# A fused retention and low-rank MLP kernel on one core: which queue stores the first 384 columns of the last output row block

## The chip, the cores and the metric

The kernel runs on one core of one Trainium2 chip. The time is that of one execution on the device, in microseconds (us); the number quoted is the median over several executions. One further execution was taken by the hardware profiler, and all durations below are from it.

## The reference

Two stages are joined. The first is a linear attention with decay, over four batches, eight heads, 768 positions and 64 values to a head; the second is a token mixer of low rank followed by an MLP.

```python
def _attn_ref(q, k, v):                      # B, H, S, D = 4, 8, 768, 64
    for t in range(S):
        state = gamma * state + k[:, :, t] (outer) v[:, :, t]
        y[:, :, t] = scale * q[:, :, t] @ state

def _moe_ref(x, U, V, w_ch1, w_ch2):         # x: 4 x 768 x 512
    h = xt @ U @ V                           # rank 32, over the 768 positions
    u = x + h.transpose(0, 2, 1)
    ch = np.maximum(u @ w_ch1, 0.0) @ w_ch2  # 512 -> 2048 -> 512
    return u + ch
```

All inputs and the output (4 x 768 x 512) are float32 in memory. The matrix products are done in bfloat16 with float32 sums.

## The kernel before, in words

The work is written out in one order by hand. Each batch's output has 768 rows, cut into six row blocks of 128 (`NCK` is 6). For a batch, `mlp_pieces` makes a list of pieces: first the products with `w_ch1` (`up`, `up_two`, lines 429 and 442), whose results pass through a relu into `gT`; then the products with `w_ch2` (`down`, line 458). For a row block `j`, sixteen matmuls, in four pieces of four, add up in one bank of PSUM. After the last of them VectorE adds `u` to the sum and puts the float32 result into `o_sb` (line 465). Then the block is stored in the output in DRAM.

`weave` puts these pieces in order, with the attention of the next batch between them. The last batch has no next one: its end is only the six row blocks of `down`, one after the other.

The stores are made in two ways. For a whole row block, `down` puts the store into a list (line 470), and `store` (line 408) issues it on GpSimd's queue (POOL) one piece later in the written order; at the end `weave` empties the list. The very last row block, batch 3 and `j` = 5, is cut in two by columns: columns 0 to 383 (`n0` = 0, `nn` = 384), then columns 384 to 511 (`n0` = 384, `nn` = 128). It is sixteen matmuls of 384 columns, a sum on VectorE and a store, then sixteen matmuls of 128 columns, a sum and a store. Before the change the first part goes the way of all others, over the list and GpSimd. The second is issued by SyncE (SP) directly, on line 468. In what follows the first part's store is called A (128 rows of 1536 bytes, 192 KB) and the second's B (128 rows of 512 bytes, 64 KB).

SyncE's queue carries the loads of q, k and v and the transposes done by DMA; its last one before the stores was issued some 37 us before the end. GpSimd's queue carries the loads of the weights and all other stores. Behind the kernel's own instructions each engine has the program's closing ones, which the profile puts on line 860: SyncE waits for the semaphores of all DMAs, every engine passes a DRAIN, and GpSimd waits until all engines have reported and then releases them, twice.

Of the kernel before, what the change touches and what calls it, by code (L numbers as in the profile page):

```python
# [16 lines left out]
def kernel(  # L17
# [13 lines left out]
    B, H, S, D = q.shape  # L31
    NCK = S // P
# [27 lines left out]
    def bank(tag, dtype=fp32):  # L60
        n_bank[0] += 1
        return psum.tile([P, 2048 // (4 if dtype == fp32 else 2)], dtype,
                         tag=tag, name=f"{tag}_{n_bank[0]}", bufs=BANKS[tag])
# [346 lines left out]
    def mlp_pieces(b):  # L410
        gT = gtp.tile([P, NM, S], bf16, tag="gT", name=f"gT_{b}")
        pieces = []
        n = [0]

        def relu(dst, src):
            n[0] += 1
            if n[0] % 3 == 0:
                nc.vector.tensor_relu(dst, src)  # L418
            else:
                nc.scalar.activation(dst, src, AF.Relu)  # L420

        def up(m, lo, sz):
            def f():
                g_p = begun.pop((b, m, lo), None)
                c0 = 3 if g_p is not None else 0
                if not c0:
                    g_p = bank("mlp")
                for c in range(c0, NCB):
                    nc.tensor.matmul(g_p[:, :sz], w1b[:, c, ts(m, P)],  # L429
                                     uTs[b][:, c, ds(lo, sz)], start=(c == 0),  # L430
                                     stop=(c == NCB - 1))
                relu(gT[:, m, ds(lo, sz)], g_p[:, :sz])
            return f

        for m in range(NM):
            pieces.append((0.864, up(m, 0, LO)))
        def up_two(m):
            def f():
                g_p = bank("mlp")
                for n in range(2):  # L440
                    for c in range(NCB):
                        nc.tensor.matmul(g_p[:, ts(n, S - LO)], w1b[:, c, ts(m + n, P)],  # L442
                                         uTs[b][:, c, LO:], start=(c == 0),
                                         stop=(c == NCB - 1))
                relu(gT[:, ds(m, 2), LO:], g_p.rearrange("p (n t) -> p n t", n=2))
            return f

        for m in range(0, NM, 2):
            pieces.append((0.864, up_two(m)))
        hold = {}  # L450

        def down(j, m0, n0=0, nn=DM):
            def f():
                if m0 == 0:
                    hold[j, n0] = bank("mlp")
                ch = hold[j, n0]
                for m in range(m0, m0 + 4):
                    nc.tensor.matmul(ch[:, :nn], gT[:, m, ts(j, P)],  # L458
                                     w2b[:, m, ds(n0, nn)],
                                     start=(m == 0), stop=(m == NM - 1))  # L460
                if m0 == NM - 4:
                    o_sb = outp.tile([P, DM], fp32, tag="o_sb",
                                     name=f"o_{b}_{j}_{n0}")[:, :nn]
                    n = ds(n0, nn)
                    nc.vector.tensor_tensor(o_sb, ch[:, :nn], us[b][:, j, n],  # L465
                                            op=ALU.add)
                    if n0:
                        nc.sync.dma_start(out=out[b, ts(j, P), n], in_=o_sb)
                    else:
                        stores.append((nc.gpsimd, out[b, ts(j, P), n], o_sb))  # L470
            return f

        for j in range(NCK):
            if (b, j) == (B - 1, NCK - 1):
                for n0, nn in ((0, 384), (384, 128)):
                    for m0 in range(0, NM, 4):
                        pieces.append((0.864 * nn / DM, down(j, m0, n0, nn)))
                continue
            for m0 in range(0, NM, 4):
                pieces.append((0.864, down(j, m0)))  # L480
        return pieces
# [383 lines left out]
```

## Time and profile before

| | |
|---|---|
| median of 3 runs | 226.62 us (225.92 to 226.64) |
| the profiled execution's own time | 224.54 us |
| its span, first to last instruction | 222.7 us |
| TensorE (PE) busy | 214.2 us, 96% of the span |
| VectorE (DVE) / ScalarE (ACT) / GpSimd (POOL) busy | 96.7 / 82.9 / 80.0 us |
| stores of whole row blocks by GpSimd | 23, 256 KB each, 2.5 us from issue to landing |
| store A, by GpSimd | 192 KB, 2.2 us from issue to landing |
| store B, by SyncE | 64 KB, 2.0 us from issue to landing |

A row of a timeline gives start, duration, engine, line and operation. A "q" behind an engine (SPq, POOLq) means the engine's sequencer, which handles semaphores, DRAINs and DMA issues; these don't count as busy time. "q0 software_dynamic" is the DMA queue that GpSimd fills and "q1 hardware_dynamic" the one that SyncE fills; both are worked off by the core's same 16 DMA engines. What lies between the span and the execution's own time, 1.84 us here, is not seen in the records.

### The profile page before, as it was taken

Reading aid. Unit: us, or ns where it says so; the run is one execution under the profiler, and the core shown is the slowest. Engines: PE = TensorE matmul, PEld = TensorE weight load, DVE = VectorE, ACT = ScalarE, POOL = GpSimd, SP = SyncE. Lnnn points to the kernel's source line nnn. Section 1 sums busy time; section 2 is a strip of 40 time slices with the busy share of each in tenths; the row PEclk is TensorE's granted clock in tenths of the full one; section 3 lists DMA queues with packets and bytes.
Section 4 is the critical chain, followed back from the end, with each engine's and each line's share of the span. In section 5 each row is a group of like instructions: output and inputs, shape, how many; then the busy total and the mean of one; then the engine's idle time right before and its main releaser. Section 6 shows DMA issues by size and latency. Waiting matters only on the chain.

```text
span 222.7 us, 4746 instructions
## 1 busy us (share of the span) xinstructions
PE 214.2 (96%) x1955; PEld 122.7 (55%) x1982; DVE 96.7 (43%) x137; ACT 82.9 (37%) x157; POOL 80.0 (36%) x115
## 2 busy tenths in 40 slices
PE   7999999999999999999999999999999999999991
PEld 2567444865665544587444444686544444864451
DVE  6678636235635346625516145251633332222111
ACT  3776454463563244565030044745120144420000
POOL 5588661125750079370101496710111100001010
PEclk9999999999999999999999999999999999999998
DMA  6999999997989996599997644411114330001211
GB/s 175 329 308 243 204 221 200 196 249 172 294 211 259 287 247 138 123 206 203 211 281 185 176 130 96 95 26 24 50 49 150 89 94 0 0 3 47 94 74 68
DMA packets 89301, 34.58 MB, mean 155 GB/s; under 512 B 71216, under 2 KB 87728, under 8 KB 89280
## 3 DMA queue, kind: packets, MB, share of 16 engines
q1 hardware_dynamic: 83152, 23.86, 46.4%
q0 software_dynamic: 6128, 10.42, 18.3%
q8 instruction: 15, 0.25, 0.5%
q14 instruction: 6, 0.05, 0.1%
HBM read 27.46 MB, written 6.29 MB: 152 GB/s over the span
## 4 chain that ended last, share of the span: by engine, by line
PE 56%; issue 31%; POOL 5%; SPq 3%; DMA 2%; DVE 1%; ACT 1%; POOLq 0%; DVEq 0%; ACTq 0%
PE mlp L458 19%; PE mlp L429 17%; PE mlp L442 6%; POOL out_dram L408 3%; SPq L106 2%; DMA in<-in_v_dram 2%; PE r L281 2%; PE r L302 1%; PE st L313 1%; PE r L297 1%; POOL vd L83 1%; PE r L639 1%; PE r L344 1%; PE r L624 1%; PE r L584 1%
## 5 line engine op out<-in xcount | busy, mean ns | idle before, releaser
L458 PE MATMUL mlp<-w2b,gT 128*128 128x512 bf16 (+2 forms) x384 | 86.6, 370 | 1.0 <-issue 0.3
L420 ACT ACTIVATE gT<-mlp 128x512 bf16<-128x512 f32 x64 | 38.1, 597 | 69.9 <-PE mlp L429 57.1
L458 PEld LDWEIGHTS <-gT 128*128 128x128 bf16 x400 | 36.9, 98 | 38.6 <-issue 0.2
L429 PE MATMUL mlp<-uT,w1b 128*128 128x512 bf16 x243 | 56.1, 379 | 0.3
L408 POOL DMA_DIRECT2D out_dram<-o x24 | 13.3, 553 | 105.0 <-DVE o L465 97.3
L418 DVE TENSOR_SCALAR gT<-mlp 128x512 bf16<-128x512 f32 x32 | 22.1, 690 | 46.2 <-PE mlp L429 23.9
L429 PEld LDWEIGHTS <-w1b 128*128 128x128 bf16 x250 | 23.6, 98 | 27.4 <-issue 0.3
L465 DVE TENSOR_TENSOR o<-mlp,u 128x512 f32<-128x512 f32 (+2 forms) x25 | 16.8, 670 | 45.1 <-PE mlp L458 44.4
L442 PE MATMUL mlp<-uT,w1b 128*128 128x256 bf16 x256 | 29.6, 273 | 0.3 <-ACT gT L420 0.2
L442 PEld LDWEIGHTS <-w1b 128*128 128x128 bf16 x256 | 24.7, 98 | 4.2 <-issue 0.4
L284 DVE TENSOR_TENSOR a<-r,mask 128x1024 bf16<-128x1024 f32 x18 | 21.2, 1219 | 7.0 <-PE r L281 7.0
L83 POOL TENSOR_TENSOR vd<-in,gk 128x512 bf16<-128x512 f32 x18 | 18.7, 1040 | 11.8 <-DMA in<-in_v_dram 11.7
L70 ACT ACTIVATE x<-r 128x512 bf16<-128x512 f32 x20 | 11.9, 596 | 26.1 <-PE r L302 25.8
L351 DVE TENSOR_TENSOR u<-r,x 128x512 bf16<-128x512 f32 (+1 forms) x16 | 14.5, 951 | 3.6 <-PE r L344 3.6
L83 POOL TENSOR_TENSOR qd<-in,gq 128x512 bf16<-128x512 f32 x12 | 12.5, 1041 | 0.0
L81 POOL CAST kd<-in 128x512 bf16<-128x512 f32 x16 | 9.7, 611 | 7.3 <-issue 6.2
L70 ACT ACTIVATE nsz<-st 64x256 bf16<-64x256 f32 x30 | 11.2, 372 | 0.3
L83 POOL TENSOR_TENSOR qp<-in,gq 128x512 bf16<-128x512 f32 x6 | 6.2, 1046 | 6.3 <-DMA in<-in_q_dram 6.3
L591 DVE TENSOR_TENSOR a<-r,mask 128x1024 bf16<-128x1024 f32 x6 | 7.3, 1222 | 2.1 <-PE r L584 2.1
L302 PE MATMUL r<-vd,a 128*128 128x64 bf16 x144 | 7.1, 193 | 0.0
L302 PEld LDWEIGHTS <-a 128*128 128x128 bf16 x144 | 6.0, 98 | 0.7
L297 PEld LDWEIGHTS <-qT 128*128 128x128 bf16 x60 | 4.6, 98 | 2.7
(109 smaller groups left out, 151.7 us busy)
## 6 DMA issues: line engine op xcount, KB each, us to landing
in<-in_k_dram SPq DMA_DIRECT2D x24, 256.0 KB, 5.0
in<-in_q_dram SPq DMA_DIRECT2D x24, 256.0 KB, 4.8
in<-in_v_dram SPq DMA_DIRECT2D x24, 256.0 KB, 4.7
out_dram<-o POOLq DMA_DIRECT2D x23, 256.0 KB, 2.5
w1b<-in_moe_w_ch_dram POOLq DMA_DIRECT2D x4, 512.0 KB, 8.1
w2b<-in_moe_w_ch_dram POOLq DMA_DIRECT2D x4, 512.0 KB, 16.1
kT<-kd SPq DMA_TRANSPOSE x12, 2.8
qT<-qd SPq DMA_TRANSPOSE x12, 2.4
```

Source lines behind the costliest of these rows:

```text
L70: nc.scalar.activation(dst, src, AF.Copy)
L83: e.tensor_tensor(dst, src, scale, op=ALU.mult)
L284: nc.vector.tensor_tensor(a, r.rearrange("p i (n m) -> p i n m", n=4), mask[:, None, None, :].to_broadcast([P, 2, 4, P]), op=ALU.mult)
L302: nc.tensor.matmul(o[:, ts(h, D)], a[:, i, hp], vb[:, h], start=(ci == 0 and h == 0), stop=True, skip_group_check=True)
L351: nc.vector.tensor_tensor(v4(us[b][:, ds(j0, nj), e]), R[g][:, :, :nj * P].rearrange("p c (j e) -> p c j e", j=nj), v4(xs[b][:, ds(j0, nj) ...
L408: eng.dma_start(out=dst, in_=src)
L418: nc.vector.tensor_relu(dst, src)
L420: nc.scalar.activation(dst, src, AF.Relu)
L429: nc.tensor.matmul(g_p[:, :sz], w1b[:, c, ts(m, P)], uTs[b][:, c, ds(lo, sz)], start=(c == 0), stop=(c == NCB - 1))
L442: nc.tensor.matmul(g_p[:, ts(n, S - LO)], w1b[:, c, ts(m + n, P)], uTs[b][:, c, LO:], start=(c == 0), stop=(c == NCB - 1))
L458: nc.tensor.matmul(ch[:, :nn], gT[:, m, ts(j, P)], w2b[:, m, ds(n0, nn)], start=(m == 0), stop=(m == NM - 1))
L465: nc.vector.tensor_tensor(o_sb, ch[:, :nn], us[b][:, j, n], op=ALU.add)
```

## The change

The condition for the direct store on SyncE is no longer "the second part of a cut row block", but "the last row block of the last batch". As only that row block is cut, B stays where it was, and A moves from the list and GpSimd's queue to SyncE's queue, ahead of B. All other stores stay on GpSimd.

```diff
                     nc.vector.tensor_tensor(o_sb, ch[:, :nn], us[b][:, j, n],
                                             op=ALU.add)
-                    if n0:
+                    if (b, j) == (B - 1, NCK - 1):
                         nc.sync.dma_start(out=out[b, ts(j, P), n], in_=o_sb)
                     else:
                         stores.append((nc.gpsimd, out[b, ts(j, P), n], o_sb))
```

## The prediction

> **What bounds the kernel now.** The page gives TensorE 96% of the span, but the change touches nothing before the last sum. So I read only the end, first in the chain of waits (start, duration, what), cut to the last microseconds:
>
> ```profile
> 215.71 0.02 POOLq L408
> 215.73 0.54 POOL out_dram L408
> 216.27 1.90 issue
> 218.17 0.56 POOLq L860
> ```
>
> The chain ends on GpSimd's side: its last store, then its sequencer on line 860, the program's close. The timeline of the end gives the order of events:
>
> ```profile
> 217.34 0.56 DVE L465 TENSOR_TENSOR o<-mlp,u 128x384 f32<-128x384 f32 x1 [1.91 <-PE mlp L458]
> 218.19 0.54 POOL L408 DMA_DIRECT2D out_dram<-o  x1 [1.92 <-DVE o L465]
> 218.23 0.29 DVE L465 TENSOR_TENSOR o<-mlp,u 128x128 f32<-128x128 f32 x1 [0.34 <-PE mlp L458]
> 218.55 0.37 SPq L468 DMA_DIRECT2D out_dram<-o  x1
> ```
>
> A's sum stands at 217.90, GpSimd issues A 0.29 us later. B's sum stands at 218.52, SyncE issues B 0.03 us later. Then line 860 alone (durations minimum, median, maximum; first and last start):
>
> ```profile
> L860 SPq EVENT_SEMAPHORE  x11: 17/28/28, 220.4 to 222.7; - x11
> L860 POOLq EVENT_SEMAPHORE  x4: 17/17/17, 221.8 to 222.6; - x4
> L860 POOLq DRAIN  x3: 46/93/3557, 218.2 to 222.2; - x3
> L860 SPq DRAIN  x3: 7/7/7, 220.9 to 222.0; - x3
> ```
>
> This is the row that matters. One GpSimd DRAIN takes 3.557 us, 218.17 to 221.73; the two others take 0.09 and 0.05 us. At 221.77 GpSimd's first semaphore instruction meets all engines. By the records behind this view SyncE passes its last DRAIN before that meeting at 221.00: it was ready 0.73 us before GpSimd. From 221.77 to the end, 222.74, is 0.97 us of closing, the same for any path.
>
> Last, the DMA engines in windows around the two stores (the last two columns are their busy share and GB/s):
>
> ```profile
> 217.90:219.30 1.40, 0.29 (x6) 0.12 (x3) 0.29 (x1) 0.00 (x0) 0.54 (x1) 1.00 0.00 0
> 219.30:219.78 0.48, 0.00 (x0) 0.00 (x0) 0.00 (x0) 0.00 (x0) 0.00 (x0) 1.00 0.96 397
> 219.78:220.15 0.37, 0.00 (x0) 0.00 (x0) 0.00 (x0) 0.00 (x0) 0.00 (x0) 1.00 0.67 194
> ```
>
> The second window holds 48 packets, all of GpSimd's queue (A); in the third 144 of 160 are SyncE's (B). So A's first packet comes 1.12 us after its issue, and B moves only when A has left the engines, 1.23 us after its own. By the records A has landed at 220.37 and B at 220.55.
>
> **The change, part by part.** *Removed from GpSimd: one DMA issue, 0.54 us, and what its DRAIN waits for.* Nothing else is queued there. The trace shows no second long DRAIN, so its cause must be bounded. It ends 3.00 us after the end of A's issue and 1.36 us after A's landing. GpSimd's last DMA is now the store of row block 4, issued 215.72 to 216.27, landed at 218.27 by the records. The DRAIN then ends at 216.27 + 3.00 = 219.27 or 218.27 + 1.36 = 219.63. Both are over a microsecond before SyncE is ready, so either way it leaves the path. If instead it waits for every DMA of the core, it stays at 221.7; I take the first reading, since the other DRAINs with no GpSimd store before them are below 0.2 us, and keep the other as a rival. What is late next is SyncE; with nothing else changed that is worth 0.73 us.
>
> *Added to SyncE: A's wait, then its issue.* SyncE is idle before it. A starts at 217.90 + 0.03 = 217.93 and, at B's price of 0.37 us (the same 128 rows), ends at 218.30. Behind the new wait stand only B and the close; B's sum stands at 218.52, so A's issue is hidden by 0.22 us, and would cost all that it takes above 0.59 us.
>
> *A's transfer.* SyncE's first packets on idle engines come 1.03 us after the issue (the load of V at 0.74) to 1.18 us (the transposes at 168.58 and 178.75), and at most 1.23 us (B). From 1.18: A's first packet at 219.11. SyncE's packets of 512 bytes take 27 ns and of 3072 bytes 127 ns in the packet records; a row of A is 1536 bytes, on the line between them 67 ns, and eight rows to each of 16 engines make 0.54 us (0.22 to 1.02 by the two rows). The engines start 0.15 us apart, as they do before, so A is through at 219.65 to 219.80.
>
> *B's transfer.* Issued at 218.55 as before; first packet 1.03 to 1.23 us later, 219.58 to 219.78. That is when A ends, so A costs B nothing; with 127 ns packets A ends by 220.28 and B is late by 0.4 us. B's packets and landing then take what they took, 0.34 us and 0.43 us: landed at 220.35 to 220.55. I take 220.45.
>
> The Trainium skill ("DMA: Bandwidth & Descriptors", Specifications) states a first byte after about 0.6 us for SyncE's queue and about 1 us for GpSimd's; no row of SyncE here is below 1.03. By that page, as an estimate, B would land near 219.9 and the change gain about 1.7 us. Against the change speaks another page of the Trainium skill ("Trainium Kernel Development and Optimization", Key Constraints): DMAs of SP, ACT and POOL share the same 16 engines, and issuing from several at once saves only the sequencer's issue time. By it the move brings nothing in data movement and gives up the parallel issue; the windows agree on the sharing (A at 397 GB/s, then B), and the rule says nothing on the DRAIN.
>
> *SyncE's list of waits.* Before, its first closing wait starts at 220.39, 0.02 us after A's landing; nine waits about 0.06 us apart and two DRAINs follow, to 221.00. So 0.62 us of list stand behind a landing. The operands in the records name the semaphores: the first wait holds that of GpSimd's last store, the eighth B's. SyncE uses eight in turn, so A takes B's old one and B the next, which is the ninth and last of the list. The other eight are then walked before B lands, and only 0.02 us, one wait and the DRAINs remain: 0.14 us. The program may order its list otherwise; at worst B is at its head, and 0.62 us remain.
>
> **The sum**, against the profiled span of 222.74: B landed 220.45, SyncE's DRAIN 220.59, GpSimd's meeting 0.05 later at 220.64 instead of 221.77: −1.13 us (−1.03 to −1.23 by B's landing). The span becomes 221.61 and that execution's 224.54 becomes 223.41. Its own time lies 2.08 us below the median of the three runs; the difference applied to the median, 226.62 − 1.13, gives 225.5.
>
> **The rivals.** *The list is walked after B's landing.* SyncE is ready at 221.07, the meeting at 221.12: −0.65 us, 225.97. For it: that is how the list ran before. Against it: the fixed order by semaphore. A's packets at 127 ns end near the same place, −0.73 us.
>
> *The DRAIN follows the last landing of any queue.* It ended 1.18 us after B's landing, the last before; B at 220.35 to 220.55 gives a DRAIN to 221.53 to 221.73, −0.2 to 0.0 us, and if the 1.36 us behind A's landing is the constant, up to +0.18: about 226.5. For it: the one long DRAIN can't tell. Against it: SyncE's own DRAINs take 7 ns, and GpSimd's started with its own last issue.
>
> *Slower: A's issue blocks SyncE.* An issue there is not always 0.37 us: a transpose took 2.07 us at 147.69, and a load with a full queue 5.81 us at 26.33. All beyond 0.59 us delays B. With B's landing 2.00 us after its issue and 0.19 us to the meeting, the new path passes the old one from an issue of 1.65 us on; at 2.07 us it is 0.4 us slower, at 5.81 us 4.2 us, 230.8. Against it: the queue has been empty for 37 us, and issues of the same 128 rows are short.
>
> *The change does less than it says*: no; only the last row block is cut, so the two conditions differ for A alone.
>
> **How the numbers follow.** Forecast 0.70, list after the landing or slow packets 0.12, DRAIN by any landing 0.13, blocked issue 0.05. About 0.3%, 0.68 us, is what a measurement of this kernel can tell from no change. The forecast lies beyond it, but by less than the spread of the three runs, 0.72 us, so some of its share falls to "same"; the list rival lies just inside, the DRAIN rival wholly. Faster 0.68, same 0.24, slower 0.08. The range goes from the forecast's far end less a spread, 226.62 − 1.23 − 0.72 = 224.7, to the DRAIN rival with its bound, 226.62 + 0.18 = 226.8. The forecast's own range is 225.0 to 226.0.
>
> **What would show it.** Right: no 3.56 us DRAIN that ends after 220; A's issue on SyncE at 0.03 us after its sum and 0.37 us long; B's issue still 0.03 us after its sum, landed by 2.0 us; SyncE's last closing wait starting with B's landing; GpSimd's meeting within 0.1 us of SyncE's DRAIN, some 2.1 us after B's issue instead of 3.2. Wrong: a GpSimd DRAIN that still ends after SyncE's, nine waits behind B's landing, B's issue late behind A's, or B's packets late behind A's.

## The result, and the profile after

The changed kernel took 224.32 us (median of ten runs, 223.51 to 226.88); the kernel before, run beside it to ten runs in all, 225.74 us (224.92 to 226.99). The ratio is 0.9931 with a 95% interval of 0.9903 to 0.9959: faster by 0.69%, some 1.6 us (0.9 to 2.2). The ratio leaves out one of the changed kernel's ten runs, 226.88 us, as it lies more than 1.5% above the fastest. The profiled execution took 223.51 us with a span of 221.7 us.

The chain of waits, cut to the last microseconds (start, duration, what), no longer has GpSimd in it:

```profile
204.96 13.65 PE mlp L458 x79
218.61 0.02 issue
218.63 0.29 DVE o L465
```

The timeline of the end:

```profile
216.13 0.54 POOL L408 DMA_DIRECT2D out_dram<-o  x1 [2.91 <-DVE o L465]
217.74 0.56 DVE L465 TENSOR_TENSOR o<-mlp,u 128x384 f32<-128x384 f32 x1 [1.91 <-PE mlp L458]
218.33 0.98 SPq L468 DMA_DIRECT2D out_dram<-o  x2
218.63 0.29 DVE L465 TENSOR_TENSOR o<-mlp,u 128x128 f32<-128x128 f32 x1 [0.33 <-PE mlp L458]
```

The two issues of SyncE stand in one row: A at 218.33, 0.03 us after its sum, B at 218.95, 0.03 us after its own. The last sum ends at 218.93; before it ended at 218.52. The 0.4 us between the two profiles arose long before the change, and so the ends are best compared from the end of the last sum on. Line 860 (durations minimum, median, maximum; first and last start):

```profile
L860 SPq EVENT_SEMAPHORE  x11: 17/28/28, 219.4 to 221.7; - x11
L860 POOLq EVENT_SEMAPHORE  x4: 17/17/17, 220.8 to 221.6; - x4
L860 POOLq DRAIN  x3: 46/93/3588, 216.1 to 221.2; - x3
L860 SPq DRAIN  x3: 7/7/7, 220.7 to 221.0; - x3
```

The long DRAIN is still there, 3.588 us long, but it starts at 216.11 and ends at 219.70, about a microsecond before SyncE's own DRAINs at 220.68 and 220.74. The meeting is at 220.77, 0.03 us after SyncE. Before, it was 0.77 us after SyncE. The DMA engines (last two columns: busy share, GB/s):

```profile
218.20:219.20 1.00, 0.40 (x8) 0.22 (x4) 0.39 (x2) 0.00 (x0) 0.00 (x0) 1.00 0.00 0
219.20:219.83 0.63, 0.00 (x0) 0.00 (x0) 0.00 (x0) 0.00 (x0) 0.00 (x0) 1.00 0.83 312
219.83:220.17 0.34, 0.00 (x0) 0.00 (x0) 0.00 (x0) 0.00 (x0) 0.00 (x0) 1.00 0.66 193
```

A moves in the second window, B in the third. A's first packet comes 0.87 us after its issue. A is slower per byte than it was on GpSimd's queue (312 against 397 GB/s) and costs nothing, since B's first packet follows at 219.83, 0.88 us after B's issue: as soon as A's own did with nothing ahead of it. The landings' records give issue to landing:

```profile
out_dram<-o SPq DMA_DIRECT2D x1, 192.0 KB, 1.9
out_dram<-o SPq DMA_DIRECT2D x1, 64.0 KB, 1.6
```

From the end of the last sum to the end of the span ("the tail" below) the kernel before took 4.21 us and the changed one 2.81 us: −1.40 us, which is 0.62% and inside the measured interval. It has three parts. The meeting now comes 0.03 us instead of 0.77 us after SyncE's DRAIN: −0.74. From the landing that SyncE's closing list waits for to its DRAIN there are 0.14 us instead of 0.63: −0.49. And that landing is B's, 1.67 us after the last sum, where it was A's, 1.85 us after it: −0.17. B itself landed 2.02 us after the last sum before the change, so it too comes 0.35 us sooner now.

### The profile page after: what moved, and what is told of

Read it like the earlier page. It is cut to its first block, busy times and chain, and to the rows that moved or that the text cites. A ratio compares the mean times of both kernels' runs of the same rounds, so it can differ in the third digit from the quotient of the medians.

```text
span 221.7 us, 4773 instructions
## 1 busy us (share of the span) xinstructions
PE 216.1 (97%) x1982; PEld 122.9 (55%) x1982; DVE 96.7 (44%) x137; ACT 82.6 (37%) x157; POOL 79.3 (36%) x114
## 4 chain that ended last, share of the span: by engine, by line
PE 87%; SPq 6%; DMA 5%; issue 0%; ACT 0%; DVE 0%; POOL 0%
PE mlp L458 38%; PE mlp L429 25%; PE mlp L442 13%; SPq L106 5%; DMA w1b<-in_moe_w_ch_dram 3%; PE r L281 2%; PE r L302 2%; DMA in<-in_q_dram 2%; PE r L297 2%; PE st L313 2%; PE r L344 1%; PE mlp L400 1%; PE mlp L271 1%; PE r L382 0%; SPq L117 0%
## 5 line engine op out<-in xcount | busy, mean ns | idle before, releaser
L458 PE MATMUL mlp<-w2b,gT 128*128 128x512 bf16 (+2 forms) x400 | 88.1, 371 | 0.0
L429 PE MATMUL mlp<-uT,w1b 128*128 128x512 bf16 x250 | 56.8, 379 | 0.0
L408 POOL DMA_DIRECT2D out_dram<-o x23 | 12.7, 554 | 103.5 <-DVE o L465 95.8
L284 DVE TENSOR_TENSOR a<-r,mask 128x1024 bf16<-128x1024 f32 x18 | 21.2, 1219 | 7.0 <-PE r L281 7.0
```

Source lines behind the costliest of these rows:

```text
L284: nc.vector.tensor_tensor(a, r.rearrange("p i (n m) -> p i n m", n=4), mask[:, None, None, :].to_broadcast([P, 2, 4, P]), op=ALU.mult)
L408: eng.dma_start(out=dst, in_=src)
L429: nc.tensor.matmul(g_p[:, :sz], w1b[:, c, ts(m, P)], uTs[b][:, c, ds(lo, sz)], start=(c == 0), stop=(c == NCB - 1))
L458: nc.tensor.matmul(ch[:, :nn], gT[:, m, ts(j, P)], w2b[:, m, ds(n0, nn)], start=(m == 0), stop=(m == NM - 1))
```

## Experiments

All edits are to the changed kernel. "SyncE is ready" when it starts its last DRAIN before the meeting. The tail and the times of the DRAIN are from one profile of each; the ratio, where one is given, is to the kernel before.

**A and B both on GpSimd.**

```diff
                     if (b, j) == (B - 1, NCK - 1):
-                        nc.sync.dma_start(out=out[b, ts(j, P), n], in_=o_sb)
+                        nc.gpsimd.dma_start(out=out[b, ts(j, P), n], in_=o_sb)
```

> A and B both stored by GpSimd, the opposite of the change. Counted from the end of the last VectorE sum to the end of the span, the kernel before took 4.21 us and the changed one 2.81 us. Theory (GpSimd's DRAIN behind its last DMA sets the end): B's issue starts 0.29 us after its sum and ends at 0.83; a DRAIN that ends 3.0 us after the issue's end gives 3.83 + 0.04 + 0.97 = 4.84 us, 0.6 us slower than before; a DRAIN that ends 1.33 us after the landing (issue + 2.0) gives 3.62 + 0.04 + 0.97 = 4.63, 0.4 us slower. Rival (the gain came only from SyncE's shorter list and B's earlier landing, the DRAIN being of no account): B lands 2.3 us after its sum, with the list behind it at most 2.9, and the close ends at 3.9 us, 0.3 us faster than before.

Measured: tail 4.61 us, ratio 1.0019 (0.9987 to 1.0051).

```profile
L860 POOLq DRAIN  x3: 51/93/3332, 221.3 to 225.1; - x3
L860 SPq DRAIN  x3: 7/7/7, 223.4 to 224.9; - x3
```

SyncE passes its DRAIN at 223.47, GpSimd's ends at 224.64, 1.17 us later: the DRAIN sets the end. It ends 2.77 us after the issue's end and 1.42 us after the landing, so the tail is that of the second reading, 4.63. The rival, with the DRAIN of no account, would have given 3.9. The evidence is the tail alone: 0.4 us more than before is under 0.2% of the time, and the ratio can't show it.

**One more DMA on SyncE, to turn the rotation of its semaphores.**

```diff
                 ch = hold[j, n0]
+                if (b, j, m0) == (B - 1, 0, 0):
+                    nc.sync.dma_start(out=scr, in_=moe_V[:1, :1])
```

> The changed kernel with one more DMA on SyncE's queue, a load of 4 bytes into a scratch tile, in the first piece of the last batch's row block 0, when SyncE is idle. It does nothing but turn the rotation of SyncE's eight semaphores by one, so that B's is the second of the closing list instead of the ninth. Theory (the list is in a fixed order, and what stands behind B's semaphore is walked after its landing): 7 waits of 0.06 us more, SyncE's DRAIN 0.56 us after B's landing instead of 0.14, from the last sum to the end 3.23 us instead of 2.81. Rival (the list follows the order of use, or its walk costs nothing): 2.81 us.

Measured: tail 3.23 us, as the list theory says, but a ratio of 1.0126 (1.0069 to 1.0183): the last sum ended at 222.36, over 3 us later than in the changed kernel. `scr`, a new tile of one float, was made for this experiment, and the loads landed later than in the changed kernel, where these medians are 4.9, 4.7 and 4.8 (last column: median us from issue to landing):

```profile
in<-in_k_dram SPq DMA_DIRECT2D x24, 256.0 KB, 5.4
in<-in_q_dram SPq DMA_DIRECT2D x24, 256.0 KB, 5.2
in<-in_v_dram SPq DMA_DIRECT2D x24, 256.0 KB, 5.4
```

The time of this run thus says nothing about the list, and it was repeated below.

**A late DMA with a late landing on GpSimd.**

```diff
                 ch = hold[j, n0]
+                if (b, j, n0, m0) == (B - 1, NCK - 1, 0, 4):
+                    load_w1(0, 512)
```

> The changed kernel with one more DMA at the end of GpSimd's queue, behind the store of row block 4: the first 512 columns of w_ch1 are loaded again (512 KB after the cast). Its landing comes late, some 4 to 8 us after the issue. It parts the two readings of GpSimd's long DRAIN. If the DRAIN ends about 3.0 us after the end of the last issue, it ends near 2 us after the last sum, and the end is set by SyncE's wait for the landing. If it ends about 1.33 us after the last landing, it ends 1.3 us after that landing, and is the last thing before the close.

```profile
220.01 0.76 POOL L229 DMA_DIRECT2D w1b<-in_moe_w_ch_dram  x1 [0.30 <-issue]
```

```profile
L862 POOLq DRAIN  x3: 46/102/7214, 220.0 to 227.7; - x3
```

The issue is over at 220.77; the load lands at 225.84. The DRAIN lasts 7.214 us, to 227.20: 6.43 us after the issue's end, 1.36 us after the landing. It follows the landing. It is GpSimd's own landing, not the last of any queue: B landed at 226.53 here, 0.67 us before the DRAIN's end, and in the changed kernel B landed 0.90 us after it.

**A 4-byte DMA on GpSimd behind A's sum.**

```diff
                         nc.sync.dma_start(out=out[b, ts(j, P), n], in_=o_sb)
+                        if n0 == 0:
+                            nc.gpsimd.dma_start(out=scr, in_=o_sb[:1, :1])
```

> The changed kernel, A and B on SyncE, with one DMA of 4 bytes on GpSimd's queue behind A's sum, where A was issued before (from A's sum in SBUF into a scratch tile). It gives back the DRAIN alone, and leaves SyncE's side as it is. From the last sum to the end, before 4.21 us, changed 2.81 us. Theory, DRAIN by the issue's end: issue about 0.3 us before the end of the last sum, 0.5 us long, DRAIN to 3.2 us, end at 4.2 us, as before: the whole gain is lost. By the landing (some 1.7 us after the issue): DRAIN to 2.7 us, end at 3.7 us: two thirds are lost. Rival (the DRAIN is not what mattered): 2.81 us.

Measured: tail 3.87 us, near the expectation by the landing (3.7), and once more a body 4 us longer with the new tile, ratio 1.0161 (1.0115 to 1.0206).

**Both again, into a tile that was there already.** `scr` became `gate0`, and its tile was left out; nothing else.

> The semaphore experiment again, with the 4-byte load going into a tile of one float that is there already (the gate of the weight loads), so that no address in SBUF moves. In the first try the tail behaved as the list theory says (3.23 us from the last sum to the end), but the work before the last sum was 3 us longer and its DMA packets of 256 bytes took 21.5 ns instead of 18.6. Theory (the new 4-byte tile had moved the addresses of all later tiles, and the DMAs into them were slower; the list costs 0.42 us): packets of 256 bytes back at 18.6 ns, tail 3.23 us, time 1.0 us below the kernel before, ratio 0.9957. Rival (the added DMA itself slows the body): packets near 21 ns and a ratio of 1.01.

Measured: tail 3.24 us, ratio 0.9954 (0.9917 to 0.9990), packets of 256 bytes at 18.8 ns, and the loads' landings back:

```profile
in<-in_k_dram SPq DMA_DIRECT2D x24, 256.0 KB, 4.6
in<-in_q_dram SPq DMA_DIRECT2D x24, 256.0 KB, 4.6
in<-in_v_dram SPq DMA_DIRECT2D x24, 256.0 KB, 4.9
```

So the place of B's semaphore in the list is worth 0.43 us, and the added DMA was not what slowed the body.

> The small GpSimd DMA behind A's sum again, into the tile that is there already. In four profiles GpSimd's long DRAIN ended 1.32 to 1.42 us after the landing of GpSimd's last DMA, whatever the DMA was (2.7 to 6.4 us after its issue's end). Theory: landing 1.5 us after the last sum, DRAIN 1.4 us later, tail 3.87 us instead of 2.81; time 0.34 us below the kernel before, ratio 0.9985: three quarters of the gain are given back by 4 bytes. Rival (SyncE's side decides, the DRAIN being hidden): tail 2.81 us, ratio 0.993.

Measured: tail 3.87 us, ratio 0.9975 (0.9940 to 1.0009).

```profile
220.21 0.52 POOL L470 DMA_DIRECT2D gate<-o  x1 [1.92 <-DVE o L465]
```

```profile
L862 POOLq DRAIN  x3: 46/112/3229, 220.2 to 223.9; - x3
L862 SPq DRAIN  x3: 7/7/13, 222.6 to 223.7; - x3
```

A and B go by SyncE here, and SyncE is ready at 222.62; the DRAIN ends at 223.42. Four bytes on GpSimd's queue give back 1.06 of the 1.40 us. They don't touch the DRAIN alone, as was expected: SyncE's list waits for their landing first and is 0.26 us later than in the changed kernel. The DRAIN ends 0.80 us later still, and sets the end.

**A on ScalarE's queue.**

```diff
-                        nc.sync.dma_start(out=out[b, ts(j, P), n], in_=o_sb)
+                        eng = nc.sync if n0 else nc.scalar
+                        eng.dma_start(out=out[b, ts(j, P), n], in_=o_sb)
```

> A on ScalarE's queue instead of SyncE's, B on SyncE as in the changed kernel. ScalarE has been idle for 20 us and its queue is empty. Theory (what the change gains is that GpSimd has no late DMA; which other queue takes A is of no account): A issued 0.03 us after its sum, B's issue and landing unchanged (1.65 us after its issue), tail 2.81 us, ratio 0.993 to the kernel before. Rival 1 (B waits behind A in SyncE's queue): B lands up to 0.1 us sooner, tail 2.7. Rival 2 (B's semaphore falls to another place of the closing list, as SyncE's rotation is one short): B takes the eighth place, one wait more behind it, tail 2.87 us.

Measured: tail 2.83 us, ratio 0.9923 (0.9885 to 0.9961), no different from the changed kernel's 0.9931.

```profile
218.65 0.38 ACTq L469 DMA_DIRECT2D out_dram<-o  x1
218.95 0.29 DVE L465 TENSOR_TENSOR o<-mlp,u 128x128 f32<-128x128 f32 x1 [0.34 <-PE mlp L458]
219.27 0.37 SPq L469 DMA_DIRECT2D out_dram<-o  x1
```

B's first packet comes 0.89 us after its issue, with A in another queue, and 0.88 us with A ahead of it in the same: being in one queue with A doesn't hold B up. B kept the ninth place of the list, so that the second rival fell too. The gain is that GpSimd has nothing late, not that SyncE has it.

**A copy of one float by GpSimd instead of a DMA**, behind A's sum, then behind B's.

```diff
+                        if n0 == 0:      # in the next one: if n0:
+                            nc.gpsimd.tensor_copy(out=gate0, in_=o_sb[:1, :1])
```

> The changed kernel with one GpSimd instruction behind A's sum that is no DMA: a copy of one float of the sum into a tile that is there already. It asks whether the long DRAIN belongs to a late GpSimd instruction of any kind. Theory (it belongs to GpSimd's last DMA, the store of row block 4): the DRAIN starts with the copy and ends by 1.4 us after that store's landing, or at once if that is past, at any rate before SyncE is ready; tail 2.81 us. Rival (any late GpSimd work brings 3 us of DRAIN): DRAIN to 2.5 us after the last sum or later, tail 3.5 us or more.

> The copy of one float by GpSimd, now behind B's sum instead of A's. With the copy behind A's sum the DRAIN ended 2.62 us after the copy's end and 2.08 us after the landing of the store of row block 4, so neither reading was settled, and the expectation that a copy is harmless was wrong: the tail was 3.27 us, not 2.81. Theory (the DRAIN has two bounds, 1.3 to 1.45 us after the last landing and some 2.65 us after GpSimd's last instruction of any kind): copy ends 0.25 us after the last sum, DRAIN to 2.9 us, tail 3.9 us. Rival (only the landing counts): the DRAIN ends within 1.9 us of the last sum, tail 2.81 to 2.9.

Behind A's sum the tail was 3.24 us (the second text has 3.27) where 2.81 was expected: a copy is not harmless. Behind B's sum it was 3.86 us.

```profile
218.81 0.18 POOL L470 COPY gate<-o 1x1 f32<-1x1 f32 x1 [2.33 <-DVE o L465]
```

```profile
L862 POOLq DRAIN  x3: 46/102/2819, 218.8 to 222.1; - x3
L862 SPq DRAIN  x3: 7/7/13, 220.5 to 221.9; - x3
```

In both the DRAIN ended 2.62 us after the copy's end, and the second time 3.10 us after the last landing of GpSimd. So the landing is not all: a late GpSimd instruction that is no DMA delays the DRAIN's end as well. Only a copy of one float was tried; what other instructions do isn't shown.

**All of the last batch's stores on SyncE**, with the copy behind A's sum (its lines are not repeated here) and without it.

```diff
-                    if (b, j) == (B - 1, NCK - 1):
+                    if b == B - 1:
```

> All six row blocks of the last batch stored by SyncE, and a copy of one float by GpSimd behind A's sum. GpSimd's last DMA is now some 40 us before the end. SyncE's rotation is five further on, so that B's semaphore has three more waits behind it in the closing list: 0.18 us more, tail 2.99 us, if the DRAIN is hidden. Theory (2.65 us of DRAIN behind any last GpSimd instruction): DRAIN to 2.26 us after the last sum, tail 3.27 us. Rival (the long DRAIN needs a DMA of GpSimd shortly before): DRAIN short, tail 2.99 us.

> All six row blocks of the last batch stored by SyncE, and nothing late on GpSimd. It asks whether still earlier rest for GpSimd brings more than the change did. Theory (once the DRAIN ends before SyncE's list, GpSimd is of no account): tail 2.81 + 0.18 us for three more waits behind B's landing = 2.99 us, ratio to the kernel before 0.994. Rival (the sums wait less, or the DRAIN still delays): tail below 2.8 us.

```profile
L862 POOLq DRAIN  x3: 46/102/2411, 220.7 to 223.7; - x3
```

With the copy: tail 2.93 us. The theory's 3.27 was wrong; the DRAIN ended 2.21 us after the copy, not 2.65, 0.12 us ahead of SyncE. So the time from the copy to the DRAIN's end is itself shorter when GpSimd's last DMA is 40 us past, though far from nothing; why was not tried.

```profile
L860 POOLq DRAIN  x3: 46/102/3418, 178.5 to 222.1; - x3
```

Without the copy: tail 2.93 us, ratio 0.9927 (0.9899 to 0.9955), no different from the changed kernel. The long DRAIN ends 37.8 us before the last sum; it ended 1.11 us after the landing of GpSimd's last store, sooner than in any other row, so the time behind a landing isn't one constant. B's semaphore is three places further from the list's end. From B's landing to SyncE's DRAIN that costs 0.19 us (0.18 expected); B landed 0.06 us sooner, so SyncE is ready 0.13 us later. Earlier rest for GpSimd brought nothing. No version tried beats the changed kernel clearly.

Over all of them but the two with the new tile, counted in us from the end of the last sum; the DRAIN's end is given also from the end of GpSimd's last instruction and from its last landing:

| kernel | GpSimd's last | DRAIN ends | from instruction | from landing | SyncE ready | tail |
|---|---|---|---|---|---|---|
| before | store A | 3.20 | 3.00 | 1.36 | 2.48 | 4.21 |
| changed | store of row block 4 | 0.77 | 3.02 | 1.32 | 1.81 | 2.81 |
| A and B on GpSimd | store B | 3.60 | 2.77 | 1.42 | 2.43 | 4.61 |
| late load | load of 512 KB | 5.23 | 6.43 | 1.36 | 4.72 | 6.23 |
| 4-byte DMA (`gate0`) | that DMA | 2.87 | 2.69 | 1.44 | 2.07 | 3.87 |
| list turned (`gate0`) | store of row block 4 | 0.77 | 3.02 | 1.32 | 2.24 | 3.24 |
| A on ScalarE | store of row block 4 | 0.76 | 3.02 | 1.32 | 1.83 | 2.83 |
| copy behind A's sum | copy | 2.24 | 2.62 | 2.08 | 1.82 | 3.24 |
| copy behind B's sum | copy | 2.86 | 2.62 | 3.10 | 1.82 | 3.86 |
| all on SyncE, copy | copy | 1.83 | 2.21 | 40.73 | 1.95 | 2.93 |
| all on SyncE | last store of the batch before | −37.80 | 2.86 | 1.11 | 1.95 | 2.93 |

In every row the tail is the later of "DRAIN ends" and "SyncE ready", and 0.98 to 1.01 us of meeting and close.

## Why the prediction was right or wrong

**The way was right, the end of the range was not.** 224.32 lies below the range's 224.7. The step that failed is the last one of the sum, 226.62 − 1.13, where the difference was applied to the median of the three runs shown. Ten runs of the same kernel, these three among them, gave 225.74, 0.88 us less. That alone moves the forecast from 225.5 to 224.6, and the range to 223.8 to 225.9. Of the 1.17 us between forecast and result, 0.88 are the base and 0.27 the end of the kernel, by the term of B's landing below; that term set right alone would still have left the result outside. That two of the three runs were among the three longest of the ten is bad luck; to take three runs for the base was the text's choice. The text had noted that the profiled execution lay 2.08 us below that median, and didn't take it as a sign that the median stood high.

**The DRAIN leaves the path**: right. The ends that the text worked out for it, 219.27 by the issue or 219.63 by the landing with the last sum at 218.52, are 0.75 and 1.11 us after that sum; 0.77 was measured. That this lies by the first figure is chance: the store of row block 4 landed 0.55 us before the last sum in this profile, against 0.26 in the one before, and the DRAIN ended 1.32 us after that landing. That it waits for GpSimd's own DMA, not for any landing, the late load shows, and so the DRAIN rival falls. The 0.73 us that the text gave for this part measured 0.74. What the text left out is that a late GpSimd instruction that is no DMA holds the DRAIN too: over 2 us for a copy of one float. It didn't matter for this change.

**SyncE's list**: right in mechanism and size. 0.14 us were worked out for the wait, the DRAINs and B as ninth of the list, and 0.14 were measured; turning the rotation gave 0.43 us back against 0.42 expected.

**A's issue and transfer**: right but for the first packet, which came 0.87 us after the issue and not 1.18. Issue 0.03 us after the sum and 0.37 us long, B's issue not delayed; 65 ns for a packet of 1536 bytes, where the line between the two rows gave 67. The rival of the blocked issue falls. (Packets of 127 ns would have made B late by 0.5 us, 220.28 less 219.78, not by the 0.4 of the text; that rival falls too.)

**B's landing**: mis-sized. 1.90 us from issue to landing were taken (1.80 to 2.00), 1.65 were measured. The term is the first packet: 1.03 to 1.23 us after the issue by the rows of a load, the transposes and B itself held up by A; 0.88 measured, below all of them. None of these rows was a near one: the transposes are another kind of DMA, the load of V reads from DRAM, and B had waited for A. The length of V's rows, 3072 bytes, is not what sets them apart: the load of 4 bytes into `gate0` also had its first packet 1.03 us after its issue, where SyncE's stores of 128 rows took 0.83 to 0.89 us in the runs without a DMA of GpSimd beside them. Why a load takes longer was not tried. This is 0.25 of the 0.27 us by which the tail's gain, 1.40, exceeds the forecast's 1.13. The page "DMA: Bandwidth & Descriptors" of the Trainium skill (Specifications) states about 0.6 us to the first byte there. No run here shows so little. The rule against the change (Key Constraints of "Trainium Kernel Development and Optimization", that issuing from several engines saves only issue time) agrees with B taking as long behind A whether A went by SyncE or by ScalarE (1.65 and 1.66 us from issue to landing). But A by GpSimd had held B's first packet to 1.23 us, and the rule was silent on the DRAIN, which decided.

## What to carry to other kernels

The end of a program is a chain of its own: from the last sum on, list what each engine still has to pass before the closing meeting, and look which comes last; here it was a DRAIN of the engine that had issued a store, 1.36 us behind the store's landing. Let the engine with the long DRAIN do its last work, a DMA or a copy, some microseconds before the end (in the changed kernel its last issue ended 2.3 us before the last sum), and let the last stores go by a queue whose close is short. Take the base for a forecast from as many runs as there are, and when the profiled execution lies far off their median, widen the range by that.

## What the runs showed of the hardware

GpSimd's closing DRAIN ended 1.32 to 1.44 us after the landing of its last DMA in the rows above where a DMA in the last microseconds was its last work, 1.11 us where that DMA was some 40 us before the end, and 2.21 to 2.62 us after a one-float copy. SyncE's DRAINs took 7 to 13 ns.

SyncE's first packet came 0.83 to 0.89 us after the issue for stores of 128 rows of 512, 1536 or 2048 bytes with no DMA of GpSimd beside them, 0.94 and 0.99 us with one of 4 bytes beside them, and 1.03 us for loads: that of V at the start and that of 4 bytes behind the last transposes.

One new tile of a single float, made ahead of the others, cost 3 to 4 us of the body in two kernels of otherwise different edits, and neither edit cost that without it. Packets of 256 bytes on SyncE's queue took 21.5 and 21.2 ns in the mean with it and 18.5 to 18.8 ns in the eleven other kernels, and those of 512 bytes 31.4 and 31.8 instead of 28.1 to 28.8. Not every packet was slower: the 256-byte packets that took 18 ns were 66% with the tile and 94% without it. The likely reason is that the later tiles' addresses moved; the addresses are not in the profile, and no run tried other sizes of the tile.
